# One written order for batch 0 of a hash-masked attention and gated MLP kernel: values up to ten chunks behind scores, exponentials in a ring of nine tiles

## The chip, the core and the metric

The kernel runs on one core of one Trainium2 chip. The metric is the device time of one execution in microseconds (us), lower is better. Engines: PE (matmul), ACT (exponential, gelu, tanh), DVE and POOL (element-wise), SP (issues most DMAs). Each engine runs its own instructions in the order in which the program issues them and waits on semaphores for the others.

## What is computed

```python
# q, k, v: (4, 8, 768, 64); proj: (64, 6)
q_bits = (q @ proj > 0); k_bits = (k @ proj > 0)      # 6 hash bits a token
mask   = bucket(q_bits) == bucket(k_bits)             # equal in all six
scores = where(mask, (q @ k.T) / sqrt(64), -1e9)
attn   = exp(scores - max); attn /= attn.sum() + 1e-9
x      = heads of (attn @ v) side by side             # (3072, 512)
g, val = x @ w_gate, x @ w_val                        # d_ff = 1536
out    = x + sigmoid(x @ w_res) * ((gelu(g) * val) @ w_out)
```

## The kernel before

**Tiling.** Two heads make a *pair* (p = 0 to 15, four pairs a batch, `HP` = 4). A pair's 768 tokens are six tiles of 128. The hash bits are put beside the 64 dimensions as ±0.5, so that one matmul with 71 rows gives a score that is pushed far down wherever the buckets differ, and no mask is applied afterwards. A pair's 2 x 36 score blocks are cut into nine *chunks* of 1024 columns (`NCH` = 9), 36 chunks a batch. Chunks 0 to 3 of a pair need its first head alone, chunk 4 both, 5 to 8 the second alone.

**A chunk.** `scores(p, c)` (L373) is two to four matmuls into a PSUM tile `sp` of 1024 columns (two such buffers, shared with the gate stage) and one exponential on ACT into a tile `e` (L385; pool of four). `values(p, c, e)` (L345) is eight matmuls of 65 columns into the accumulator `av` of a head (two buffers); at the end of a head `preset` (L323) adds a tiny uniform term, and `finish(p, hi)` (L299) divides on DVE into `x_tok`. A finished pair is transposed into `x_sb`, by a DMA on SP's queue (L310) or on PE (`x_turn`, L335).

**Preparing a pair.** Loads on SP (`load`, `load_v`); `tr` (DVE transpose for the hash, L194); `cast` (POOL, into one of four tiles `nat`); `hash_mm` (PE, fp32, L205); `hash_tok` and `bits` (DVE, partly POOL, L215 and L224); then either `turn_pe` and `turned` (PE transposes into a PSUM bank, DVE copy out: pairs 1 to 3) or `turn` (a DMA transpose on SP, L248: pairs 4 to 15), which gives `aug`, the operand of the scores. `vals_a` and `vals_s` prepare the values on POOL.

**Stages.** Per batch: attention (36 slots), then `gate_val(b)` (L403): for m = 0 to 11, eight matmuls with `wg`, eight with `wv` (L399), gelu on ACT (L416), one multiplication on DVE into `hh` (L419). `project(b)` (L425; L431, L445) is a generator whose matmuls are put into the slots of the next batch's attention, or at the end by themselves. Side work of each slot stands in two dictionaries, `side_pe` (issued behind the slot's scores) and `side_work` (issued behind its values); side work of the gate stage stands by m in `gv_work`, issued behind the multiplication of that m. Values come `LAG` = 2 chunks behind scores. The order inside a stage is the order of issue; nothing reorders it later.

**Batch 0** is not covered by a previous batch's projection: its slots hold scores, values, and the preparation of pairs 1 to 3, and its loads come first. In its gate stage pairs 4 to 7 are prepared: `bits` and `turn` of pair 4 and 5 behind m = 0, 1, 2, 4, `tr` of pair 7 behind m = 3 and 5, the hash of pairs 6 and 7 on PE behind m = 6, their `turn`s behind m = 7 to 10. Both loads of pair 7 have been issued in slots 28 and 31 of batch 0. Weight loads are issued on POOL's queue, nine in slots up to 35 and behind m = 0, the others by m = 7.

Of the kernel before, what the change touches and what calls it, by code (L numbers as in the profile page):

```python
# [14 lines left out]


@with_exitstack
def kernel(
# [12 lines left out]
    nc = tc.nc  # L31
# [73 lines left out]
    load(1, 0)  # L105
    load_v(0)
    load(1, 1)
    for p in range(2, 4):
        load_v(p - 1)
        load(p, 0)  # L110
        load(p, 1)
# [76 lines left out]
    t32, hsum, htok = {}, {}, {}  # L188

# [7 lines left out]
    def hash_mm(jobs, dhs=(0, 1), hs_=(0, 1)):  # L197
        if jobs[0] not in hsum:
            hsum[jobs[0]] = mm_ps.tile([P, HT, 32], FP32, tag="r", name="hs")
# [8 lines left out]

    def hash_tok(jobs, psum=False):
        n = 32 * len(jobs)  # L210
        if psum:
            ht = mm_ps.tile([P, HT, 32], FP32, tag="f", name="htp")
        else:
            ht = sm_pool.tile([P, HT, 32], FP32, tag="ht", name="ht")
        nc.vector.transpose(ht[:n].rearrange("p c n -> p (c n)"),  # L215
                            hsum[jobs[0]][:n].rearrange("p c n -> p (c n)"))
        for j, x in enumerate(jobs):
            htok[x] = (ht, j)

    def bits(p, side, engs=(nc.vector,)):  # L220
        x = (p, side)
        ht, j = htok.pop(x)
        for a in range(4):
# [6 lines left out]
    def hash_one(p, side, hi, pool, tag):  # L230
        hs = pool.tile([P, 2, T, 32], FP32, tag=tag, name="hs1")
# [6 lines left out]
    def bits_one(p, side, hi):  # L238
# [4 lines left out]
                                hs[:, 1, :, 0:NBITS], 0.0, 0.5, op0=ALU.is_gt, op1=ALU.subtract)  # L243

# [7 lines left out]

    def turn_pe(p, side, hi, tag=None, pool=mm_ps):
# [3 lines left out]
        pt = pool.tile([P, T, P], BF16, tag=tag or "rf"[side], name="pt")  # L257
# [4 lines left out]
    def turned(p, side, hi, eng, t0=0, t1=T):  # L262
        dst = aug[p, side][0:KA, hi * T + t0:hi * T + t1, :]
        pt = pts[p, side, hi][0:KA, t0:t1]
        if eng is nc.scalar:
            nc.scalar.activation(dst, pt, AF.Copy)
        else:
            eng.tensor_copy(dst, pt)

# [29 lines left out]
    def finish(p, hi):  # L299
# [4 lines left out]
        o = av.pop((p, hi))  # L304
        rec = sm_pool.tile([P, T], FP32, tag="rec", name="rec")
# [3 lines left out]
        if hi == 1 and (0 < b < B - 1 or hp < HP - (2 if b == 0 else 1)):  # L309
# [6 lines left out]
    def opened(p, hi):  # L316
        if (p, hi) in av:
            return
        av[p, hi] = av_ps.tile([P, T + 1, D + 1], FP32, tag="av", name="av")
# [15 lines left out]
    def x_turn(b, hp):  # L335
        pt = mm_ps.tile([P, T, P], BF16, tag="f" if b == 0 else "r", name="pt")
# [8 lines left out]
    def values(p, c, e):  # L345
        va = vaug[p]
        for i in range(2):
# [12 lines left out]
            if (2 * c + i + 1) % NCH == 0:  # L360
                if p < HP:
                    preset(p, hi)
                if (p, hi) not in late:
                    finish(p, hi)

    pending = []
    late = ((0, 0), (0, 1), (1, 0))
# [5 lines left out]
    def scores(p, c):  # L373
# [10 lines left out]
        e = e_pool.tile([P, 1024], BF16, tag="e", name="e")  # L384
# [5 lines left out]
    hidden = {}  # L390
# [12 lines left out]
    def gate_val(b, begun, beside):  # L403
        for m in range(KF):
            ps = []
            for i, w in enumerate((wg, wv)):
# [5 lines left out]
                if m == 0 and i == 1:  # L412
# [4 lines left out]
            if m == 0:  # L417
# [7 lines left out]
    def project(b):  # L425
        hh = hidden[b]
        for t in range(T):
            last = b == B - 1 and t == T - 1
            rps = mm_ps.tile([P, DMODEL], FP32, tag="r", name="rps")
# [8 lines left out]
            for k0, k1 in ((0, 3), (3, 4)) if last else ((0, KM),):  # L438
                cs = slice(k0 * P, k1 * P)
                if b < B - 1:  # L440
                    fps = mm_ps.tile([P, DMODEL], FP32, tag="f", name="fps")
# [22 lines left out]
    tr(0, 0, 1, 2)  # L464
# [44 lines left out]
    for p in range(HP, NPAIR):  # L509
        for hi, s in enumerate((9 * p - (p % HP == 0), 9 * p + 5)):  # L510
            at(s - 2, lambda p=p, hi=hi: opened(p, hi))
# [23 lines left out]


    at(0, lambda: bits_one(0, 0, 1), lambda: tr(1, 0), lambda: bits_one(0, 1, 1))
    pe(0, lambda: hash_one(0, 1, 1, av_ps, "av"))
    at(1, lambda: tr(1, 1))
    pe(2, lambda: turn_pe(0, 0, 1, "av", av_ps), lambda: turn_pe(0, 1, 1))  # L540
    at(2, lambda: turned(0, 0, 1, nc.vector))
    at(2, lambda: turned(0, 1, 1, nc.vector, 0, 2), lambda: turned(0, 1, 1, nc.vector, 2, T))
    at(2, lambda: tr(2, 0))
    hash_pe((1,), 4, (4,))
    turns_pe(1, (6, 6, 8, 9))
    at(6, lambda: finish(0, 0), lambda: tr(2, 1))
    at(8, lambda: tr(3, 0))
    at(9, lambda: tr(3, 1))
    at(11, lambda: finish(0, 1))
    at(5, lambda: vals_a(1))  # L550
    at(7, lambda: vals_s(1))
    for side in range(2):
        at(4 + side, lambda side=side: cast(2, side, nc.gpsimd))
        at(9 + side, lambda side=side: cast(3, side, nc.gpsimd))
    hash_pe((2, 3), 13, (13, 16))
    turns_pe(2, (15, 15, 17, 18))
    at(15, lambda: finish(1, 0))
    at(13, lambda: vals_a(2))
    at(15, lambda: vals_s(2))
    turns_pe(3, (22, 22, 23, 24))  # L560
    at(18, lambda: vals_a(3))
    at(22, lambda: vals_s(3))
    pe(30, lambda: x_turn(0, HP - 2))
    for i in range(6):
        at(11 + 3 * i, load_w)
    for m in (0, 0, 4, 5, 6, 7):
        gv(0, m, load_w)
    loads(0, (3, "v"))

# [4 lines left out]
    for b in range(B - 1):  # L574
# [3 lines left out]
        for j, (x, y) in enumerate(zip(xs, ys)):  # L578
            at(s0 + 24 + 2 * j, lambda x=x: tr(*x))
            at(s0 + 25 + 2 * j, lambda x=x: cast(*x, nc.gpsimd))  # L580
            if j < 2:
                at(s0 + 32 + 2 * j, lambda y=y: tr(*y))
            loads(s0 + (6 if b == 0 else 2) + 4 * j, (x[0], "qk"[x[1]]))
            loads(s0 + (22 if b == 0 else 18) + 3 * j, (y[0], "qk"[y[1]]))
        gv(b, 0, lambda p0=p0: tokens((p0, p0 + 1), True))
# [97 lines left out]
```

## Time and profile before

| | |
|---|---|
| time, median of 3 runs | 346.99 us (346.71 to 347.24) |
| profiled execution: first to last instruction (its span) | 344.9 us |
| median less that span: what lies around it | 2.1 us |
| PE, ACT, DVE, POOL busy | 97%, 60%, 56%, 25% of the span |
| first and last exponential of batch 0 | 8.49 us, 47.47 us (end) |
| gate stage of batch 0, first and last full stretch on PE | 52.25 us to 82.56 us |
| granted PE clock | 1.00 throughout |

The profiled execution has no time of its own beside its span; its own time is taken as the span plus the 2.1 us. Columns of a timeline row: start, us taken, engine, line, operation, output and input, how many, and in brackets the engine's idle time before it with what ended it. Rows of ACT overlap a little when they follow each other closely. A busy PE is not PE at its peak, as the ends of matmuls are modelled: where PE waits is read from the chain of waits.

### The profile page before, as it was taken

The page shows a single profiled execution, that of the slowest core. Times are in us where ns is not written, and L with a number is a line of the kernel's source. Part 1 is how long each engine was busy: PE and PEld are TensorE (multiplying, and loading weights), DVE is VectorE, ACT ScalarE, POOL GpSimd, SP SyncE. Part 2 cuts the span into 40 slices and gives each one's busy share as a digit, 9 for nine tenths or more (in the row PEclk, how much of TensorE's full clock was granted, in tenths as well). Part 3 has the DMA queues.
Part 4 walks back from the last instruction along what each step waited for, and adds up shares of the span by engine and source line. Part 5 has one row for each costly group of instructions (what it writes and reads, how often), then busy time and mean ns, then how long its engine had stood idle before and what let it go on. Part 6 is the DMA issues. An engine that isn't in the chain of part 4 may idle for free.

```text
span 344.9 us, 7549 instructions
## 1 busy us (share of the span) xinstructions
PE 334.2 (97%) x3064; PEld 204.3 (59%) x3112; DVE 191.4 (56%) x403; ACT 206.7 (60%) x232; POOL 86.3 (25%) x162
## 2 busy tenths in 40 slices
PE   7999999999999999999999999999999999999994
PEld 5667665655666655655666665655566665656442
DVE  7877757755345856757344784747244444333333
ACT  3789973226999962224999982323999984223110
POOL 4779940371055000270044100242030000000000
PEclk9999999999999999999999999999999999999999
DMA  7979999999375833528366642626330220000022
GB/s 224 376 62 219 205 276 217 197 139 193 103 188 172 204 106 78 102 38 149 82 193 188 231 115 65 128 48 113 72 100 32 55 55 30 32 1 0 32 77 76
DMA packets 71171, 42.90 MB, mean 124 GB/s; under 512 B 49504, under 2 KB 68192, under 8 KB 71136
## 3 DMA queue, kind: packets, MB, share of 16 engines
q1 hardware_dynamic: 64720, 37.17, 42.9%
q0 software_dynamic: 6336, 5.24, 10.8%
q8 instruction: 24, 0.39, 0.4%
q14 instruction: 11, 0.09, 0.1%
q10 hardware_dynamic: 80, 0.00, 0.0%
HBM read 29.36 MB, written 6.29 MB: 103 GB/s over the span
## 4 chain that ended last, share of the span: by engine, by line
PE 88%; ACT 4%; DVE 2%; DMA 2%; issue 2%; SPq 1%; POOL 0%; DVEq 0%; ACTq 0%
PE sp L399 36%; PE fps L445 18%; PE sp L380 15%; PE av L354 8%; PE rps L431 6%; ACT e L385 4%; PE hs L205 3%; DMA ld<-in_k_dram 2%; PE pt L259 1%; DVE o L451 1%; DVE nat L224 0%; SPq L96 0%; DVE o L448 0%; DVE ht L215 0%; DVE hh L419 0%
## 5 line engine op out<-in xcount | busy, mean ns | idle before, releaser
L385 ACT ACTIVATE e<-sp 128x1024 bf16<-128x1024 f32 x144 | 143.6, 1027 | 13.5 <-PE sp L380 8.0
L416 ACT ACTIVATE gt<-sp 128x768 bf16<-128x768 f32 x48 | 38.9, 811 | 92.5 <-PE sp L399 92.5
L380 PE MATMUL sp<-aug,aug 71*128 71x256 bf16 (+1 forms) x384 | 86.1, 325 | 1.1 <-ACT e L385 0.6
L445 PE MATMUL fps<-wo,hh 128*128 128x512 bf16 (+2 forms) x274 | 74.7, 369 | 1.6
L419 DVE TENSOR_TENSOR hh<-gt,sp 128x768 bf16<-128x768 bf16 x48 | 45.8, 954 | 50.1 <-PE sp L399 46.1
L399 PE MATMUL sp<-x_sb,wv 128*128 128x512 bf16 (+1 forms) x379 | 70.6, 325 | 0.4 <-DVE hh L419 0.2
L399 PE MATMUL sp<-x_sb,wg 128*128 128x256 bf16 (+1 forms) x373 | 70.4, 324 | 0.7
L354 PEld LDWEIGHTS <-e 128*128 128x128 bf16 x1152 | 53.3, 97 | 28.9 <-issue 1.2
L354 PE MATMUL av<-va,e 128*128 128x65 bf16 x1152 | 58.7, 193 | 0.1
L399 PEld LDWEIGHTS <-wv 128*128 128x128 bf16 x384 | 37.6, 98 | 25.1 <-issue 0.3
L399 PEld LDWEIGHTS <-wg 128*128 128x128 bf16 x384 | 36.8, 98 | 26.2 <-issue 2.3
L445 PEld LDWEIGHTS <-hh 128*128 128x128 bf16 x300 | 27.4, 97 | 22.7 <-issue 0.2
L448 DVE SCALAR_TENSOR_TENSOR o<-th,fps 128x512 f32<-128x512 f32 (+2 forms) x25 | 16.6, 666 | 36.6 <-PE fps L445 31.0
L380 PEld LDWEIGHTS <-aug 71*128 71x128 bf16 x384 | 29.4, 97 | 10.9 <-issue 2.2
L184 POOL TENSOR_SCALAR nat<-ld 128x768 bf16<-128x768 f32 (+1 forms) x16 | 13.8, 861 | 78.0 <-DMA aug<-nat 74.6
L281 POOL TENSOR_TENSOR v<-ldv 128x384 f32<-128x384 f32 x16 | 16.0, 999 | 67.7 <-DMA ldv<-in_v_dram 67.6
L194 DVE STREAM_TRANSPOSE t<-ld 128x768 f32<-128x768 f32 (+1 forms) x34 | 31.0, 916 | 1.4 <-DMA ld<-in_q_dram 0.7
L333 DVE COPY av<-av 128x390 f32<-128x390 f32 x24 | 13.6, 567 | 29.8 <-PE av L329 29.8
L431 PE MATMUL rps<-wr,x_sb 128*128 128x512 bf16 x90 | 25.3, 378 | 0.2
L435 ACT ACTIVATE th<-rps 128x512 f32<-128x512 f32 x24 | 14.2, 594 | 18.4 <-PE rps L431 18.4
L224 DVE TENSOR_SCALAR nat<-htp 32x72 bf16<-32x72 f32 x96 | 21.9, 229 | 1.8
L307 DVE TENSOR_TENSOR x_tok<-av,rec 128x384 bf16<-128x384 f32 x32 | 17.8, 557 | 1.1
(61 smaller groups left out, 190.7 us busy)
## 6 DMA issues: line engine op xcount, KB each, us to landing
ldv<-in_v_dram SPq DMA_DIRECT2D x16, 384.0 KB, 5.4
out_dram<-o SPq DMA_DIRECT2D x23, 256.0 KB, 2.0
ld<-in_q_dram SPq DMA_DIRECT2D x15, 384.0 KB, 5.4
ld<-in_k_dram SPq DMA_DIRECT2D x15, 384.0 KB, 6.2
wg<-in_moe_w_gate_dram POOLq DMA_DIRECT2D x4, 384.0 KB, 10.2
wv<-in_moe_w_val_dram POOLq DMA_DIRECT2D x4, 384.0 KB, 12.2
wo<-in_moe_w_out_dram POOLq DMA_DIRECT2D x3, 512.0 KB, 6.9
wr<-in_moe_w_res_dram POOLq DMA_DIRECT2D x1, 512.0 KB, 14.9
```

The costliest lines, as they stand in the source:

```text
L194: nc.vector.transpose(t32[p, side][:, sl].rearrange("p c h n -> p (c h n)"), raw[p, side][:, sl].rearrange("p c d -> p (c d)"))
L224: engs[a % len(engs)].tensor_scalar(nat_of(x)[32 * a:32 * a + 32, :, D:D + NBITS], ht[32 * j:32 * j + 32, :, NBITS * a:NBITS * (a + 1)], 0 ...
L307: nc.vector.tensor_mul(x_tok[b][:, hp, :, hi * D:(hi + 1) * D], o[:, 0:T, 0:D], rec.unsqueeze(2).to_broadcast([P, T, D]))
L354: nc.tensor.matmul(av[p, hi][:, qt, :], e[:, off:off + P], va[:, hi, jt, 0:D + 1], start=first, stop=(p >= HP and jt == T - 1), skip_group ...
L380: nc.tensor.matmul(sp[:, off:off + nq * P], ks[0:KA, hi * T + jt, :], qs[0:KA, hi * T + qt0:hi * T + qt0 + nq, :], start=True, stop=True)
L385: nc.scalar.activation(e, sp, AF.Exp, scale=float(ALPHA))
L399: nc.tensor.matmul(sp[:, c0:c1], w[:, kk, bass.ts(m, P)], xs[:, kk, c0:c1], start=(kk == 0), stop=(kk == KM - 1))
L416: nc.scalar.activation(gt, sp[:, 0:S], AF.Gelu)
L419: nc.vector.tensor_mul(hidden[b][:, m, :], gt, ps[1][:, 0:S])
L431: nc.tensor.matmul(rps, x_sb[b][:, kk, t, :], wr[:, kk, :], start=(kk == 0), stop=(kk == KM - 1))
L445: nc.tensor.matmul(fps[:, cs], hh[:, m, bass.ts(t, P)], wo[:, m, cs], start=(m == 0), stop=(m == KF - 1))
L448: nc.vector.scalar_tensor_tensor(o[:, cs], th[:, cs], 1.0, fps[:, cs], op0=ALU.add, op1=ALU.mult)
```

## The change

Batch 0 no longer runs in the loop over slots. A list of named pieces, `ORDER`, is read from front to back, and each name issues one piece: `sN` scores of chunk N, `vN` its values, `finPH` the finish, `ldPS`/`lvP` loads (S is 0 for q, 1 for k), `trPS`, `csPS` (cast), `hN0` to `hN3` (quarters of a hash), `tkN` (tokens), `btPS` (bits), `tpPSH`/`tdPSH` (turn on PE and copy), `tuPS` (turn by DMA), `vaP`/`vsP`, `wN` (weight load), `xtP` (x_turn), `opP`/`prP`/`rpP` (open, preset, repeat), `g0`, `g1` (first three quarters of m = 0). `BESIDE` is the same for the gate stage of batch 0, by m. The exponentials of batch 0 go into the tile `hh`, which that batch's gate stage fills later: a ring of nine pieces of 1024 columns, where there were four tiles `e`. PSUM banks of `mm_ps`, with fixed names before, are handed out by a list of free ones. Batches 1 to 3 keep their slots.

```diff
+FIRST_LOADS = [(1, "q"), (0, "v"), (1, "k"), (2, "q"), (2, "k"), (1, "v"), (2, "v"), (3, "k"), (3, "q")]
+HASHES = [(0, (1,)), (1, (2, 3)), (2, (4, 5)), (3, (6, 7))]
+ORDER = """
+trq trk s0 tdq tdk hoq bo0 ho bo1 s1 tr10 s2 tr11 tp011 td011a td011b tp001 v0 td001 v1 s3 h00 h01
+s4 cs21 h02 h03 s5 tr20 ld41 ld40 s6 v2 v3 v4 tr21 s7 tk0 bt10 bt11 tp100 tp110 td100 td110 cs20 s8
+ld50 tp111 s9 tr30 tr31 tp101 td101 fin00 s10 lv3 v5 v6 v7 v8 fin01 s11 va1 vs1 lv4 va2 s12 ld60 h10
+h11 h12 h13 ld61 td111 s13 cs31 v9 s14 v10 v11 v12 s15 cs30 tk1 bt20 bt21 tp210 s16 td210 tp200
+td200 v13 fin10 bt31 s17 ld51 va4 v14 s18 tr50 tp201 w0 w1 w2 bt30 td201 s19 v15 vs2 s20 tp211 cs41
+td211 s21 v16 v17 cs40 s22 tr61 v18 v19 tr40 w3 s23 va3 tp310 td310 tr60 s24 v20 tp300 td300 ld70
+s25 vs3 v21 tp301 td301 s26 vs4 fin11 s27 v22 v23 fin20 tr41 s28 v24 v25 s29 tp311 td311 s30 v26
+fin21 lv6 s31 lv5 cs50 v27 s32 cs51 v28 v29 s33 xt2 v30 tr51 s34 w4 w5 w6 v31 fin30 s35 gelu v32 v33
+v34 g0 v35 fin31 g1 xt3 h20 h21 h22 w7 op40
+"""
+BESIDE = [
+    "h23 tk2 bt41",
+    "tu41 cs61 bt40",
+    "bt50",
+    "tu40 cs60 ld71 tr71",
+    "tr70",
+    "tu50 bt51 w8 w9",
+    "",
+    "w10",
+    "h30 h31 h32 h33 tu51 cs71 tk3 bt60 bt61 tu60 tu61",
+    "pr40 rp40 bt71 tu71",
+    "bt70",
+    "w11 cs70 tu70",
+]
...
-        pt = pool.tile([P, T, P], BF16, tag=tag or "rf"[side], name="pt")
+        pt = pool.tile([P, T, P], BF16, tag=tag or take((p, side, hi)), name="pt")
...
-            rps = mm_ps.tile([P, DMODEL], FP32, tag="r", name="rps")
+            rps = mm_ps.tile([P, DMODEL], FP32, tag=take(), name="rps")
...
-        e = e_pool.tile([P, 1024], BF16, tag="e", name="e")
+        if p < HP:
+            if 0 not in hidden:
+                hidden[0] = hh_pool.tile([P, KF, S], BF16, tag="hh", name="hh")
+            n = (p * NCH + c) % RING
+            e = hidden[0].rearrange("p m s -> p (m s)")[:, n * 1024:(n + 1) * 1024]
+        else:
+            e = e_pool.tile([P, 1024], BF16, tag="e", name="e")
...
     for side in range(2):
         tr(0, side, 0, 1)
         hash_one(0, side, 0, av_ps, "av")
-    tr(0, 0, 1, 2)
     cast(0, 0, nc.scalar, 0, 1)
     cast(0, 1, nc.gpsimd, 0, 1)
     bits_one(0, 0, 0)
     turn_pe(0, 0, 0)
     fill(2, 256)
-    turned(0, 0, 0, nc.scalar)
     bits_one(0, 1, 0)
+    turned(0, 0, 0, nc.scalar, 0, 4)
     turn_pe(0, 1, 0)
-    hash_one(0, 0, 1, av_ps, "av")
-    tr(0, 1, 1, 2)
     turned(0, 1, 0, nc.vector, 0, 2)
-    turned(0, 1, 0, nc.vector, 2, T)
...
+    for name in ORDER.split():
+        first.pop(name)()
...
+            for m, names in enumerate(BESIDE):
+                for name in names.split():
+                    gv(b, m, first.pop(name))
...
-    for s in range(LAST):
+    gate_val(0, begun)
+    mlp.append(project(0))
+    for s in range(NSLOT, LAST):
```

More of the change, by code (lines that the diff above doesn't have):

```diff
@@ L104 @@
     load_head(0, 1, 1, nc.sync)
[L105 to L111, printed above, removed]
+    for what in FIRST_LOADS:
+        load_v(what[0]) if what[1] == "v" else load(what[0], "qk".index(what[1]))
     warm = const.tile([P, P], BF16, name="warm")
@@ L211, in hash_tok @@
         if psum:
[L212 removed]
+            ht = mm_ps.tile([P, HT, 32], FP32, tag=take(("ht", ht_of(jobs))), name="htp")
         else:
@@ L222, in bits @@
         ht, j = htok.pop(x)
+        n, what = ht_left.pop(id(ht))
+        if n > 1:
+            ht_left[id(ht)] = (n - 1, what)
+        else:
+            give(what)
         for a in range(4):
@@ L558, with job @@
[L558 to L568, printed above, removed]
+    first = {}
+    def job(name, fn):
+        first[name] = fn
+    held = []
+    for c in range(HP * NCH):
+        job(f"s{c}", lambda c=c: held.append(scores(*divmod(c, NCH))))
+        job(f"v{c}", lambda: values(*held.pop(0)))
```

196 lines of the change are left out of this document (125 added, 71 removed).

## The prediction

> **What bounds the kernel now.** I read the page first, then the chain of waits, then the timelines of ACT, DVE, PE and SP in the two stages that the change rewrites.
>
> ```profile
> PE 88%; ACT 4%; DVE 2%; DMA 2%; issue 2%; SPq 1%; POOL 0%; DVEq 0%; ACTq 0%
> L385 ACT ACTIVATE e<-sp 128x1024 bf16<-128x1024 f32 x144 | 143.6, 1027 | 13.5 <-PE sp L380 8.0
> ```
>
> Over the whole span PE carries the chain, and ACT's exponentials only 4% of it. All of that share lies in batch 0, so batch 0 has to be read by itself. ACT's timeline of batch 0, with the first gelu behind it:
>
> ```profile
> 8.49 4.08 ACT L385 ACTIVATE e<-sp 128x1024 bf16<-128x1024 f32 x4 [0.89 <-PE sp L380]
> 13.39 1.02 ACT L385 ACTIVATE e<-sp 128x1024 bf16<-128x1024 f32 x1 [0.82 <-PE sp L380]
> 14.95 1.94 ACT L385 ACTIVATE e<-sp 128x1024 bf16<-128x1024 f32 x2 [0.54 <-PE sp L380]
> 17.60 5.64 ACT L385 ACTIVATE e<-sp 128x1024 bf16<-128x1024 f32 x6 [0.71 <-PE sp L380]
> 23.72 1.02 ACT L385 ACTIVATE e<-sp 128x1024 bf16<-128x1024 f32 x1 [0.49 <-PE sp L380]
> 25.30 1.94 ACT L385 ACTIVATE e<-sp 128x1024 bf16<-128x1024 f32 x2 [0.55 <-PE sp L380]
> 27.99 6.55 ACT L385 ACTIVATE e<-sp 128x1024 bf16<-128x1024 f32 x7 [0.76 <-PE sp L380]
> 34.80 2.04 ACT L385 ACTIVATE e<-sp 128x1024 bf16<-128x1024 f32 x2 [0.26 <-PE sp L380]
> 37.00 10.47 ACT L385 ACTIVATE e<-sp 128x1024 bf16<-128x1024 f32 x11 [0.16 <-PE sp L380]
> 51.39 0.81 ACT L416 ACTIVATE gt<-sp 128x768 bf16<-128x768 f32 x1 [1.16 <-PE sp L399]
> ```
>
> These 36 exponentials run from 8.49 to 47.47 us, so the last one starts at 37.00 + 10.47 − 1.03 = 46.44. In the undisturbed run of eleven their pitch is (10.47 − 1.03)/10 = 0.944 us; inside the run of seven it is (6.55 − 1.03)/6 = 0.92. Eight times ACT waited for scores: 0.82 + 0.54 + 0.71 + 0.49 + 0.55 + 0.76 + 0.26 + 0.16 = 4.29 us, of which 3.47 fall behind the fifth exponential (13.39). Check: 31 × 0.944 + 3.47 = 32.7 us against the 33.05 from 13.39 to 46.44. So batch 0 is exponentials at full pitch plus gaps in which PE did something else first. The chain within batch 0 says what:
>
> ```profile
> 11.66 0.84 PE hs L205 x8
> 12.51 0.35 PE av L354 x8
> 12.86 0.44 PE sp L380 x3
> 18.18 0.35 PE pt L259 x6
> 22.05 0.79 PE hs L205 x16
> 23.63 0.83 PE hs L205 x16
> 27.17 0.17 PE av L326
> 27.89 0.24 PE av L354 x8
> 49.81 1.11 PE hs L205 x24
> 50.92 0.45 PE sp L399 x2
> ```
>
> In PE time a chunk's scores cost 0.44, its values 0.24, a preset 0.17, a turn of six transposes 0.35, half a four-job hash about 0.8. The waits of ACT sit where such pieces stand between two chunks' scores. After the last exponential PE needs until 50.92 for the rest of batch 0; from there the gate stage keeps it full.
>
> **Part 1: the order of batch 0.** Moving values does not remove PE work; it moves it out of the crowded slots. Between two scores PE may spend 0.944 − 0.44 = 0.50 us before it is the later of the two. The second `sp` buffer adds a little once: an exponential starts about 0.6 us after its scores begin (12.86 to 13.39 is 0.53), so PE may lag 0.3 to 0.4 before ACT waits. I went through ORDER with the prices above, carrying the lag. Most slots hold 0.24 to 0.6 us of other work and pay the lag back. Five do not: two quarters of a hash behind s4 (0.8), three values and a preset behind s6 (0.9), two turns behind s7 (0.7, which also wait on DVE's tokens and bits), four values and a preset behind s10 (1.15), and four quarters behind s12 (1.6). Their excess over 0.50 plus the lag is about 0.1, 0.2, 0.25, 0.35 and 0.7: 1.6 us of waiting in place of 3.47, a gain of 1.9. From s14 on nothing exceeds it, where the old order still lost 0.55, 0.76, 0.26 and 0.16.
>
> The fifth exponential: in the old order a hash (11.66), then values (12.51), then its scores (12.86). Both values now stand ahead of the hash, so the scores come right behind it, 0.35 earlier. The hash itself keeps its time, since it waits for POOL's copies of `projw`, which stay behind the same cast:
>
> ```profile
> 10.73 0.88 POOL L144 COPY projw<-projn 32x12 f32<-32x12 f32 x4
> 5.03 0.58 DVE L194 STREAM_TRANSPOSE t<-ld 128x384 f32<-128x384 f32 x1 [0.67 <-DMA ld<-in_q_dram]
> 5.53 0.35 DVE L240 STREAM_TRANSPOSE hs<-hs 128x192 f32<-128x192 f32 x1
> ```
>
> Ahead of that, the DVE transpose that waited for its load until 5.03 no longer stands before the first bits (5.53), so the first scores come up to 0.6 earlier; but the second halves' transposes, bits and copies then come later on DVE, and they are what the fifth chunk needs. I count 0.3 gained at the fifth exponential; the ends are 0.6 and −0.5. Sum at the end of batch 0: 1.9 + 0.3 = **2.2 us**. With the pitch 0.92 it is 31 × 0.024 = 0.7 more (2.9); if the gaps stay as large as they are, only 0.3. The tail from the last exponential to the gate stage keeps its pieces.
>
> [...]
>
> **Part 2: the load of pair 7's k.** BESIDE issues `ld71` on SP's queue only behind m = 3, and `tr71`, which reads it, on DVE directly behind it. On SP it stands behind `tu41` and `tu40`; `tu40` waits for `bt40`, the bits behind m = 1. On DVE, queued behind `tr71` is the multiplication of m = 4, and for that PE waits with the `wv` matmuls of m = 5, because it frees their buffer.
>
> ```profile
> 53.73 0.93 DVE L224 TENSOR_SCALAR nat<-htp 32x72 bf16<-32x72 f32 x4
> 56.10 0.95 DVE L224 TENSOR_SCALAR nat<-htp 32x72 bf16<-32x72 f32 x4
> 60.32 0.95 DVE L419 TENSOR_TENSOR hh<-gt,sp 128x768 bf16<-128x768 bf16 x1 [0.66 <-PE sp L399]
> 61.19 0.97 DVE L194 STREAM_TRANSPOSE t<-ld 128x768 f32<-128x768 f32 x1
> 62.92 0.95 DVE L419 TENSOR_TENSOR hh<-gt,sp 128x768 bf16<-128x768 bf16 x1 [0.76 <-PE sp L399]
> 63.95 1.46 PE L399 MATMUL sp<-x_sb,wv 128*128 128x512 bf16 x8
> ```
>
> In the old trace's times (all of this shifts together): bits of m = 0 end at 54.66, those of m = 1 at 57.05. The multiplication of m = 3 starts at 60.32, a transpose behind it at 61.19, that of m = 4 at 62.92 and ends at 63.87; PE wants the buffer at 63.95. There is no slack there. A transpose of 0.97, less the 0.08 by which DVE's rows overlap (60.32 + 0.95 against 61.19), holds the next one off by 0.89, so the load must have landed by 62.92 − 0.89 = 62.03. When does it?
>
> ```profile
> 54.82 3.77 SPq L248 DMA_TRANSPOSE aug<-nat  x1
> 82.10 1.43 SPq L248 DMA_TRANSPOSE aug<-nat  x1
> 83.58 0.91 SPq L78 DMA_DIRECT2D ld<-in_q_dram  x1
> ld<-in_q_dram SPq DMA_DIRECT2D x1, 384.0 KB, 5.8
> DMA to landing us min/median/max: 4.0/4.0/4.0
> DMA to landing us min/median/max: 3.4/3.4/3.4
> DMA to landing us min/median/max: 7.1/11.4/16.1
> q0 software_dynamic: 1852, 1.58, 98.4%
> ```
>
> A turn leaves SP 0.16 us after its bits (54.66 to 54.82) and occupies SP for 1.43 us when the DMAs are quiet (82.10), 3.77 when they are not (54.82). So `tu40` goes at 57.2 and `ld71` at 58.7. A load right behind a turn landed 5.8 us after issue in batch 1 (83.58; the fourth line) and 4.0 in batch 2 (the fifth, the load at 163.6); one at 98.3 took 3.4; among weight loads they took 7.1 to 16.1 (the seventh, loads from 24 to 39 us). Landing at 62.1, 62.7 or 64.5 stalls PE by 0.1, 0.7 or 2.5 us, once, and PE is full from there to the end of the stage, so it is lost. I take 1.5, between the two that stood behind a turn.
>
> **Part 3: edits at nothing.** The exponentials in `hh`: its first piece is overwritten by m = 0, long after the values that read it (v27), and its last one by m = 11, after v35; if the order did not cover it, one value step (0.24). The banks from a list: the order of rps and fps stays alternating. The hash of pairs 6 and 7 moves from m = 6 to m = 8: PE pays it there instead; behind it DVE has tokens and two sets of bits, 0.6 + 2 × 0.95 = 2.5 us, while PE's hash and m = 9 take over 3; no stall, or 0.3 if it slips. Weight loads go out later: the last two pairs of `wg`, `wv` slices only near s34, needed at m = 6 and 9; `wr` and `wo` behind cs60, needed in batch 1, some 15 us on. The last of these is the nearest: POOL can ask for `wr` when `tu40` has landed and cs60 is done, some 5 to 8 us behind 57.2;
>
> ```profile
> wr<-in_moe_w_res_dram POOLq DMA_DIRECT2D x1, 512.0 KB, 14.9
> ```
>
> with the 14.9 us that it took among the other weights it lands by 62 to 65 + 15 = 80 at the latest, and the gate stage ends at 82.5. If it were later still, the first slots of batch 1 would wait for the difference.
>
> **Sum.** Span 344.9 − 2.2 + 1.5 = 344.2; with the 2.1 us around it 346.3, against the median 346.99.
>
> **The rivals.**
>
> *Full gain.* The load lands by 62.1, as the load at 98.3 would (3.4), and batch 0 gains 2.2 to 2.9: 346.99 − 2.5 = 344.5. For it: DMAs have less to do in batch 0. Against: the two loads behind a turn took longer. [...] Chance 0.20.
>
> *Late load, slower than before.* When `tu41` leaves, slices of the weights asked for at s34 are still in flight, as in the old trace, where the software queue had 98.4% of the engines from 50 to 60 us. Then `tu41` takes 3.77 (to 58.6), `tu40` 1.43 (60.1), `ld71` lands at 65.9 and PE stalls 3.9 us: 346.99 − 2.2 + 3.9 = 348.7; if both turns and the load are slowed, 5 us and more, 350. It decides from a stall of 2.2, a landing at 64.3. For it: the row of 54.82. Against: only the four slices asked for last are behind, and no loads. Chance 0.20.
>
> *Batch 0 does not tighten.* DVE, with `tr20`, `tr21` and tokens in one row behind s5, or a POOL waiting for `lv4` (which SP issues only behind the DMA of pair 0's x), holds the turns up, and the gaps move rather than go: gain 0.5, stall 1.5: 348.0. Chance 0.15; the ring and the lag of ten chunks then do nothing, since nothing but PE's order was to be gained by them.
>
> **How the numbers follow.** My case (gain 2.2, stall 1.5) has 0.45 and spans 345.0 to 347.6 by itself. What a measurement here tells from no change is about 0.2%, 0.7 us, so faster means under 346.3, which is where my own figure lies. Faster: half of my case 0.23 and the full gain 0.20, 0.43. Same: 0.16 of my case and 0.04 of the last, 0.20. Slower: 0.06, 0.20 and 0.11, 0.37. The range 344.4 to 349.0 leaves out the best part of the full gain (0.08) and the worst of the late load (0.1).
>
> **What would show it.** Right: in the new trace the last exponential of batch 0 starts near 44.2, ACT's gaps sum to about 2 us and sit behind chunks 4 to 12; in the gate stage DVE's transpose of m = 3 waits for the DMA of `ld`, and PE has one pause of about 1.5 us before the `wv` matmuls of m = 5. Wrong: gaps behind s14 (ACT is not held by PE's order), no pause at m = 5 (rival one), a pause above 2.2 us (rival two), or pauses at another m or in the first slots of batch 1, which I have priced at nothing.

## The result, and the profile after

| | before | after |
|---|---|---|
| time, median (runs) | 346.82 us (12, 346.42 to 347.46) | 346.1 us (12, 345.6 to 347.14) |
| ratio | | 0.9982 (95%: 0.9974 to 0.999) |
| span of the profiled execution | 344.9 us | 344.4 us |
| first and fifth exponential | 8.49, 13.39 | 8.50, 13.89 |
| first gelu of batch 0 | 51.39 | 50.85 |
| table load behind the gate stage of batch 0 | 82.12 | 82.17 |

The changed kernel is faster by 0.18%. The forecast was 346.3. One slow run, 352.66 us in the experiment e2_bits_behind, is left out of its ratio. Read between the marks of the table, the half microsecond of span is the sum of four parts, and no part has the size that was forecast: the fifth exponential comes 0.50 later, the stretch from there to the first gelu is 1.04 shorter (38.00 to 36.96), the gate stage 0.59 longer (30.73 to 31.32), and everything behind it 0.55 shorter (262.78 to 262.23).

First the timeline of ACT after the change, to be held against the one of before in the prediction (columns: start, us taken, engine and line, what, how many; in brackets the idle time before it and what ended it):

```profile
8.50 1.02 ACT L459 ACTIVATE hh<-sp 128x1024 bf16<-128x1024 f32 x1 [1.04 <-PE sp L448]
10.44 1.94 ACT L459 ACTIVATE hh<-sp 128x1024 bf16<-128x1024 f32 x2 [0.92 <-PE sp L448]
12.58 1.02 ACT L459 ACTIVATE hh<-sp 128x1024 bf16<-128x1024 f32 x1 [0.19 <-PE sp L448]
13.89 1.02 ACT L459 ACTIVATE hh<-sp 128x1024 bf16<-128x1024 f32 x1 [0.29 <-PE sp L448]
15.21 5.83 ACT L459 ACTIVATE hh<-sp 128x1024 bf16<-128x1024 f32 x6 [0.29 <-PE sp L448]
21.45 1.94 ACT L459 ACTIVATE hh<-sp 128x1024 bf16<-128x1024 f32 x2 [0.41 <-PE sp L448]
23.86 8.55 ACT L459 ACTIVATE hh<-sp 128x1024 bf16<-128x1024 f32 x9 [0.47 <-PE sp L448]
33.78 13.16 ACT L459 ACTIVATE hh<-sp 128x1024 bf16<-128x1024 f32 x14 [1.37 <-PE sp L448]
...
50.85 0.81 ACT L489 ACTIVATE gt<-sp 128x768 bf16<-128x768 f32 x1 [1.16 <-PE sp L472]
```

Seven waits behind the fifth exponential have become four, 0.29 + 0.41 + 0.47 + 1.37 = 2.54 us in place of 3.47. But more than half of that is one wait of 1.37 ahead of chunk 22, in a part of the order for which the prediction saw none; a gap behind s14 was the first sign that it had named for being wrong. DVE's timeline ahead of it, and PE's row:

```profile
28.07 0.90 DVE L282 TENSOR_SCALAR nat<-ht 32x72 bf16<-32x72 f32 x2
28.99 0.98 DVE L240 STREAM_TRANSPOSE t<-ld 128x768 f32<-128x768 f32 x1
29.98 2.21 DVE L282 TENSOR_SCALAR nat<-ht 32x72 bf16<-32x72 f32 x4
32.22 1.02 DVE L329 COPY aug<-pt 71x768 bf16<-71x768 bf16 x2
...
33.30 0.39 PE L448 MATMUL sp<-aug,aug 71*128 71x512 bf16 x1 [1.20 <-DVE aug L329]
```

PE stops in the middle of chunk 22's scores, because the copy of `td211` (the second of the two at 32.22) is not there. On DVE that copy stood behind half of `bt31`, `tr50` and `bt30`. The four bits of `bt30` took 2.21 us. A narrower window gives the last two of them alone, and POOL's timeline what ran beside:

```profile
30.60 1.59 DVE L282 TENSOR_SCALAR nat<-ht 32x72 bf16<-32x72 f32 x2
...
30.34 0.75 POOL L193 DMA_DIRECT2D wg<-in_moe_w_gate_dram  x1
31.10 1.02 POOL L346 TENSOR_TENSOR v<-ldv 128x384 f32<-128x384 f32 x1
```

They end at 32.19, and POOL's addition beside the last one ends at 31.10 + 1.02 = 32.12.

Second, the load that was moved behind m = 3. The timelines of SP, DVE and PE in the gate stage, and the line of that load's landing:

```profile
54.27 3.58 SPq L308 DMA_TRANSPOSE aug<-nat  x2
57.91 0.89 SPq L107 DMA_DIRECT2D ld<-in_k_dram  x1
...
62.10 0.98 DVE L240 STREAM_TRANSPOSE t<-ld 128x768 f32<-128x768 f32 x1 [1.36 <-DMA ld<-in_k_dram]
63.00 0.92 DVE L492 TENSOR_TENSOR hh<-gt,sp 128x768 bf16<-128x768 bf16 x1
...
62.11 1.46 PE L472 MATMUL sp<-x_sb,wg 128*128 128x512 bf16 x8
63.97 1.46 PE L472 MATMUL sp<-x_sb,wv 128*128 128x512 bf16 x8 [0.39 <-DVE hh L492]
```

```profile
DMA to landing us min/median/max: 4.2/4.2/4.2
```

DVE's transpose waits 1.36 for the load, the multiplication of m = 4 comes behind it, and the `wv` matmuls of m = 5 start 1.86 behind the `wg` matmuls where the matmuls before and after are 1.30 apart: 0.56 us lost, at the place that was named. That eats the 0.54 won in batch 0, so that both kernels end the gate stage at the same time.

### The profile page after: what moved, and what is told of

It is laid out like the page before. It is cut to its first block, busy times and chain, and to the rows that moved or that the text cites. A ratio compares the mean times of both kernels' runs of the same rounds, so it can differ in the third digit from the quotient of the medians.

```text
span 344.4 us, 7546 instructions
## 1 busy us (share of the span) xinstructions
PE 333.5 (97%) x3064; PEld 204.3 (59%) x3112; DVE 191.7 (56%) x404; ACT 206.2 (60%) x232; POOL 85.6 (25%) x162
## 4 chain that ended last, share of the span: by engine, by line
PE 90%; DVE 3%; ACT 3%; issue 1%; DMA 1%; SPq 0%; POOL 0%; DVEq 0%; ACTq 0%; POOLq 0%
PE sp L472 34%; PE fps L518 18%; PE sp L448 17%; PE av L421 9%; PE rps L504 6%; PE hs L251 3%; ACT hh L459 2%; DMA ld<-in_k_dram 1%; PE pt L320 1%; PE wps L174 1%; DVE nat L282 1%; PE hs L293 1%; DVE aug L329 1%; ACT gt L489 0%; SPq L308 0%
## 5 line engine op out<-in xcount | busy, mean ns | idle before, releaser
L459 ACT ACTIVATE e<-sp 128x1024 bf16<-128x1024 f32 x108 | 109.0, 1028 | 8.0 <-PE sp L448 2.8
L472 PE MATMUL sp<-x_sb,wv 128*128 128x256 bf16 (+1 forms) x378 | 70.6, 325 | 0.7 <-DVE hh L492 0.4
L421 PEld LDWEIGHTS <-e 128*128 128x128 bf16 x864 | 40.2, 97 | 25.1
L421 PE MATMUL av<-va,e 128*128 128x65 bf16 x864 | 43.4, 193 | 0.0
L459 ACT ACTIVATE hh<-sp 128x1024 bf16<-128x1024 f32 x36 | 34.4, 1026 | 5.1 <-PE sp L448 5.0
L521 DVE SCALAR_TENSOR_TENSOR o<-th,fps 128x512 f32<-128x512 f32 (+2 forms) x25 | 16.7, 666 | 36.9 <-PE fps L518 30.0
L210 POOL CAST nat<-ld 128x768 bf16<-128x768 f32 (+1 forms) x17 | 13.3, 783 | 39.7 <-DMA aug<-nat 38.8
```

Of the source, the lines that this page charges most:

```text
L421: nc.tensor.matmul(av[p, hi][:, qt, :], e[:, off:off + P], va[:, hi, jt, 0:D + 1], start=first, stop=(p >= HP and jt == T - 1), skip_group ...
L459: nc.scalar.activation(e, sp, AF.Exp, scale=float(ALPHA))
L472: nc.tensor.matmul(sp[:, c0:c1], w[:, kk, bass.ts(m, P)], xs[:, kk, c0:c1], start=(kk == 0), stop=(kk == KM - 1))
L521: nc.vector.scalar_tensor_tensor(o[:, cs], th[:, cs], 1.0, fps[:, cs], op0=ALU.add, op1=ALU.mult)
```

## The experiments

Each kernel is the changed one with one edit, the last two with two and three; all were timed against the kernel before on their own chip (346.81, 346.94 and 347.02 us there), and ratios are against that. The changed kernel was not timed again beside them, so where an edit is set against it, the two ratios are compared (its own is 0.9982). Batch 0 shifts with the landing of the first loads (the first exponential came between 7.91 and 9.49), so stages are compared by their lengths. The changed kernel's marks are: fifth exponential to first gelu 36.96, fifth exponential to table load 68.28.

### The load

**e1_load_early** issues it where the second load of batch 0's end stands:

```diff
-fin21 lv6 s31 lv5 cs50 ...                 # ORDER
+fin21 lv6 s31 lv5 ld71 cs50 ...
-    "tu40 cs60 ld71 tr71",                  # BESIDE, m = 3
+    "tu40 cs60 tr71",
```

> The changed kernel with one name moved: ld71, the load of pair 7's k, goes out behind lv5 (slot 31) and no longer behind m = 3. If the pause of 0.56 us before the wv matmuls of m = 5 is that load and is lost for good: no wait of DVE's transpose on a DMA there, gate stage of batch 0 back to 30.3 us, 0.56 us less than the changed kernel, about 345.5. If instead something behind it is late anyway (the turns of pair 5, the weight slices that the load now meets): the pause moves to another m and the time stays at 346.1.

344.91 us (5 runs), ratio 0.9951 (0.9939 to 0.9963). PE's timeline at m = 5, and ACT's table load:

```profile
61.67 1.46 PE L472 MATMUL sp<-x_sb,wg 128*128 128x512 bf16 x8
62.97 1.46 PE L472 MATMUL sp<-x_sb,wv 128*128 128x512 bf16 x8
...
81.17 1.28 ACT L459 ACT_TABLE_LOAD   x1
```

No pause: 1.30 from one to the next. The late load is the cause: in the ten traces that keep it PE waits at this place (0.27 to 0.67 us), in the three with the early one it does not. The ratio falls by 0.0031, 1.1 us, which is more than the pause. From the fifth exponential (13.79) to the table load it is 67.38, 0.90 less: 0.56 by the pause, 0.34 because the wait at chunk 22 was 1.03 in this execution. There the two bits of `bt31` on DVE took 0.56 us, where the row at 28.07 above has 0.90.

### The wait ahead of chunk 22

Theory: DVE's queue sets it. Four edits change what stands in it or how long it takes.

**e2_bits_behind** moves `tr50` and `bt30` on DVE behind the copy that PE wants:

```diff
-... s18 tr50 tp201 w0 w1 w2 bt30 td201 s19 v15 vs2 s20 tp211 cs41 td211 s21
+... s18 tp201 w0 w1 w2 td201 s19 v15 vs2 s20 tp211 cs41 td211 tr50 bt30 s21
```

> The changed kernel with tr50 and bt30 moved on DVE from slot 18 to behind td211 (slot 21), so that the two copies for which the scores of chunk 22 wait no longer stand behind them. If DVE's queue makes ACT's gap of 1.37 us at 33.78: the gap shrinks to 0.2 or less, the last exponential of batch 0 starts 1.2 us earlier (44.7), time about 344.9. If PE's own work is as full as ACT's there: the gap comes back in smaller pieces by slot 35, time 345.6 to 346.1.

347.71 us (11 runs), ratio 1.0027 (1.0016 to 1.0038): slower than the changed kernel, which both sides had missed. ACT's timeline shows where the gain went:

```profile
37.71 2.02 ACT L459 ACTIVATE hh<-sp 128x1024 bf16<-128x1024 f32 x2 [1.09 <-PE sp L448]
40.22 7.49 ACT L459 ACTIVATE hh<-sp 128x1024 bf16<-128x1024 f32 x8 [0.49 <-PE sp L448]
```

The wait at chunk 22 is gone, and 1.09 + 0.49 come back at chunks 26 and 28: the same DVE work now stands ahead of pair 3's turns. Here work moved within a full queue moved the wait. The trace does not account for the whole loss: first gelu is 37.34 behind the fifth exponential, 0.38 more than in the changed kernel, while the ratio is 0.0045 higher, 1.6 us. The traced execution was one of the quicker ones (347.08), and four of the ten runs in the ratio had a mean granted clock of 0.994 or 0.995, where it had 0.997; what they lost, and where, no trace shows.

**e3_vsum_early** takes POOL's additions away from beside the bits:

```diff
-... s17 ld51 va4 v14 s18 ... s19 v15 vs2 s20
+... s17 ld51 vs2 va4 v14 s18 ... s19 v15 s20
```

> The changed kernel with one name moved: vs2 (POOL's sums over the values of pair 2) from slot 19 to ahead of va4 in slot 17, where POOL waited 1.7 us for a load. bt30 then no longer runs beside POOL's additions. If DVE's small operations are slowed by POOL's tensor operations beside them (four took 2.21 us where four took 0.93 elsewhere, the last one 1.06 while POOL's addition took 1.02): bt30 takes 1.2 us or less, the gap of 1.37 shrinks to about 0.4, time about 345.2. If they are slowed by POOL's weight loads or by themselves: bt30 stays near 2.2 and the time at 346.1.

346.96 us (11 runs), ratio 1.0006 (0.9997 to 1.0015), worse than the changed kernel's 0.9982. DVE's and POOL's rows, and PE's wait:

```profile
30.18 2.22 DVE L282 TENSOR_SCALAR nat<-ht 32x72 bf16<-32x72 f32 x4
...
30.76 0.75 POOL L193 DMA_DIRECT2D wg<-in_moe_w_gate_dram  x1
31.50 0.84 POOL L210 CAST nat<-ld 128x768 bf16<-128x768 f32 x1
...
33.51 0.39 PE L448 MATMUL sp<-aug,aug 71*128 71x512 bf16 x1 [1.45 <-DVE aug L329]
```

The bits are as slow (2.22), with a DMA issue and a cast beside them instead of the additions. So it is not one POOL operation that slows them. The two bits of `bt31` ahead of them took 1.14 here, 0.24 more than in the changed kernel, and ACT's wait at chunk 22 is 1.62, 0.25 more.

**e11_tokens_psum** leaves POOL's other work as it is and puts the input of those bits into PSUM; all bits of pairs 2 and 3 then stand on DVE, four more in all:

```diff
-job(f"tk{n}", lambda ps=ps: tokens(ps, ps[0] >= HP))
+job(f"tk{n}", lambda ps=ps: tokens(ps, ps[0] >= 2))
-... (nc.vector,) if side == 0 or p >= HP else (nc.gpsimd, nc.vector)
+... (nc.vector,) if side == 0 or p >= 2 else (nc.gpsimd, nc.vector)
```

> The hash tokens of pairs 2 and 3 go to PSUM instead of SBUF, and their bits stand wholly on VectorE (GpSimd did half of the k side's). [...] Then every set of four bits of pairs 2 and 3 takes 0.90 to 0.98 us, pair 3's q bits too (2.21 in the changed kernel), though GpSimd's operations lie beside it as before; the gap behind chunk 21 shrinks from 1.37 to below 0.7 and the time is 345.3 to 346.1. Rival: the bits are held by GpSimd's work wherever their input lies (the output is in SBUF still): single bits of 0.4 to 1.06 us remain, and with two more bits a set on VectorE the time is 346.1 to 347.

346.68 us (11 runs), ratio 0.9993 (0.9984 to 1.0001). The groups of bits by line between 23 and 33 us, those of pairs 2 and 3 (columns: how many, ns shortest/median/longest, first and last start), first of the changed kernel, then of this one, and of this one its last eight bits, POOL's rows beside them, and a row of PE:

```profile
L282 DVE TENSOR_SCALAR nat<-ht x12: 185/202/1061, 23.9 to 31.1; 32x72 bf16<-32x72 f32 x12
```

```profile
L282 DVE TENSOR_SCALAR nat<-htp x16: 221/228/239, 24.6 to 32.3; 32x72 bf16<-32x72 f32 x16
```

```profile
29.56 0.98 DVE L282 TENSOR_SCALAR nat<-htp 32x72 bf16<-32x72 f32 x4
...
31.55 0.96 DVE L282 TENSOR_SCALAR nat<-htp 32x72 bf16<-32x72 f32 x4
...
29.89 0.75 POOL L193 DMA_DIRECT2D wv<-in_moe_w_val_dram  x1
...
31.39 1.01 POOL L346 TENSOR_TENSOR v<-ldv 128x384 f32<-128x384 f32 x1
...
32.55 0.50 PE L320 MATMUL pt<-ident,nat 128*71 128x128 bf16 x6 [0.77 <-DVE nat L282]
```

The place of the input decides here: with a DMA issue and an addition on POOL beside them no bit takes over 239 ns, where single bits with their input in SBUF took up to 1061. The time is not better than the changed kernel's, since DVE has more bits and PE now waits for those (0.77 at 32.55); first gelu 37.12 behind the fifth exponential. The first of the two times expected was missed at its upper end, the rival's met, but for another reason than the rival's.

**e7_bits_pool** takes `bt30` off DVE: POOL makes pair 3's q bits, directly behind its half of the k bits.

```diff
-td200 v13 fin10 bt31 s17 ... w0 w1 w2 bt30 td201
+td200 v13 fin10 bt31 bt30 s17 ... w0 w1 w2 td201     # bt30 on nc.gpsimd
```

> The changed kernel with all four parts of bt30 on POOL, right behind its parts of bt31, where POOL stood idle for 1.7 us; none left on DVE. If ACT's gap of 1.37 us is DVE's queue (bt30 of 2.21 us ahead of the copies for chunk 22): the copies come at 30.0, the gap goes to 0.2 or less and does not come back at chunk 27, last exponential of batch 0 at 44.7, time about 344.9. If the weight loads, 0.4 later on POOL, or PE's own work hold it then: 345.5 to 346.1.

345.04 us (6 runs), ratio 0.9947 (0.9932 to 0.9962). ACT:

```profile
13.88 1.02 ACT L459 ACTIVATE hh<-sp 128x1024 bf16<-128x1024 f32 x1 [0.29 <-PE sp L448]
...
23.84 21.71 ACT L459 ACTIVATE hh<-sp 128x1024 bf16<-128x1024 f32 x23 [0.47 <-PE sp L448]
...
49.47 0.81 ACT L489 ACTIVATE gt<-sp 128x768 bf16<-128x768 f32 x1 [1.16 <-PE sp L472]
```

23 exponentials without a wait, the whole second part of batch 0, at (21.71 − 1.03)/22 = 0.94 us each; first gelu 35.59 behind the fifth exponential, 1.37 less than in the changed kernel, which is the size of the wait. DVE's queue was the cause.

### How far the values lag

**e5_lag2** puts each values step two chunks behind its scores, **e12_lag3** at most three; in both the finish of pair 1's second head stands earlier, because the two accumulators then need it. In the order as it is the distance reaches five (`v5` behind `s10`, `v22` behind `s27`); title and prediction overstated it with ten.

```diff
-... s10 lv3 v5 v6 v7 v8 fin01 s11 ... s21 v16 v17 cs40 s22 ...
+... s10 lv3 v8 fin01 s11 ... s21 cs40 v19 s22 ...      # two chunks, every values step so
+... s10 lv3 v7 v8 fin01 s11 ... s21 cs40 v18 s22 ...   # at most three
```

> The changed kernel with the values of batch 0 two chunks behind the scores, as before, instead of up to ten (fin11 moved forward to suit); everything else in its place. If the lag is what batch 0 lives on: slots with turns or hashes take a value step more, ACT's gaps behind the fifth exponential grow from 2.8 us to well over 3.5, and the time is 346.8 or more. If the gaps are set by DVE's queue and by the places of hashes and turns, and the values fit anywhere: gaps grow by 0.2 to 0.4 us (the prediction's own prices give 0.2), time 346.1 to 346.5.

> Values at most three chunks behind their scores instead of up to five; all else in the order as it is. Theory: what the distance buys is that copies, bits and finishes on VectorE are not queued behind work that waits for late scores and values; two chunks cost 5 us, so three cost something between, 347 to 350 us, and ScalarE's gaps behind the fifth exponential sum to 3 to 4.5 us (2.54 in the changed kernel, 5.14 with two). Rival, the price of the prediction (values are only PE time, 0.24 us each, and cost where a slot is overfull): 346.1 to 346.4, gaps of 2.5 to 2.8.

Two chunks: 351.1 us (4 runs), ratio 1.0115 (1.0102 to 1.0128). Three: 347.52 us (12 runs), ratio 1.0015 (1.0005 to 1.0024). The changed kernel has 0.9982. ACT's waits behind the fifth exponential sum to 0.54 + 0.20 + 1.20 + 1.71 + 0.25 + 1.24 = 5.14 with two and 0.29 + 0.95 + 1.17 + 0.84 = 3.25 with three, against 2.54. Of three, ACT's rows and one of PE:

```profile
23.82 8.75 ACT L459 ACTIVATE hh<-sp 128x1024 bf16<-128x1024 f32 x9 [0.95 <-PE sp L448]
...
38.38 9.50 ACT L459 ACTIVATE hh<-sp 128x1024 bf16<-128x1024 f32 x10 [0.84 <-PE sp L448]
...
37.57 0.28 PE L421 MATMUL av<-va,hh 128*128 128x65 bf16 x4 [0.52 <-DVE x_tok L373]
```

With three, first gelu comes 38.28 behind the fifth exponential, 1.32 later than in the changed kernel. The wait ahead of chunk 13, at the hash of pairs 2 and 3, is 0.95 for 0.47, but the 0.41 ahead of chunk 11 is gone; that exponential comes 10.30 behind the fifth, where it came 9.97 behind it. One values step, `v9`, has moved into that full slot, so these 0.33 are near the prediction's own price of 0.24. The rest comes behind chunk 22, and most of it is not PE's time: ACT waits 0.84 ahead of chunk 26, because a values step waits for an accumulator that a finish on DVE has not yet given back. With two chunks something else comes in. PE's longest wait, and the five microseconds behind it by the view of windows (window, its length, busy time and instructions of five engines, then granted clock, DMA share, GB/s):

```profile
35.36 0.39 PE L448 MATMUL sp<-aug,aug 71*128 71x512 bf16 x1 [1.74 <-DVE aug L329]
```

```profile
36.00:41.00 5.00, 5.00 (x53) 3.74 (x52) 3.24 (x6) 3.52 (x4) 4.68 (x10) 0.66 1.61 137
37.00:40.00 3.00, 3.00 (x22) 1.93 (x21) 1.93 (x4) 1.81 (x2) 2.84 (x7) 0.50 1.35 135
```

A wait of 1.74 that ends at 35.36, and from 36.9 to 40.3 PE runs at half its clock; ACT's waits of 0.25 and 1.24 are of that stretch. What it withholds is 5 × (1 − 0.66) = 1.7 us of PE at full clock, or 3.4 us at half. All four runs of this kernel have a mean clock of 0.989 to 0.993. So of the 3.27 by which first gelu is farther from the fifth exponential (40.23), at most about half belongs to the half clock and the rest to the distance itself.

### The start and the loads

**e4_old_start** gives the changed kernel the start of before, with the second halves' transposes and one hash ahead of the first exponential:

```diff
-trq trk s0 tdq tdk hoq bo0 ho bo1 s1 tr10 ...
+s0 ho bo0 tr10 bo1 s1 ...                  # tr and hash_one back ahead of s0
```

> The changed kernel with the start of the kernel before: second halves of pair 0 transposed and hashed ahead of the first scores, copies whole. If the new start costs the first five exponentials (second one 1.03 us later, fifth 13.89 against 13.39): the fifth comes at 13.1 to 13.4, time about 345.5. If the fifth hangs on POOL's copies of projw, which came 0.8 later because the load of pair 1's q landed later: it stays near 13.8 and the time at 346.1.

346.66 us (12 runs, 345.41 to 349.06), ratio 1.0003 (0.9985 to 1.002): not told apart from before or from the changed kernel. The profiled execution was the longest of these; it and the next (348.69) had a mean granted clock of 0.992 and 0.993, the other ten at least 0.997. The fifth exponential and PE's wait at chunk 22, then the window behind that wait:

```profile
14.33 1.02 ACT L459 ACTIVATE hh<-sp 128x1024 bf16<-128x1024 f32 x1 [0.29 <-PE sp L448]
...
34.12 0.49 PE L448 MATMUL sp<-aug,aug 71*128 71x512 bf16 x1 [1.58 <-DVE aug L329]
```

```profile
34.00:38.00 4.00, 3.88 (x38) 2.79 (x39) 2.88 (x5) 2.12 (x3) 3.99 (x8) 0.57 1.28 192
```

The fifth exponential stands 14.33 − 9.49 = 4.84 behind the first, as in the kernel before (4.90), where the changed one takes 5.39. The old start is quicker by 0.5 between these marks, but its first exponential came at 8.97 and 9.49 in two traces (8.49 in the kernel before), where the new start had it between 7.91 and 9.23; so part of that may have been paid ahead of it. And the wait at chunk 22 was 1.58 in this execution, and the clock fell behind it as in e5_lag2: 4 × (1 − 0.57) = 1.7 us withheld. Behind waits of 1.20, 1.33 and 1.45 (the changed kernel, three chunks, e3_vsum_early) the clock of batch 0 stayed at 1.00.

**e8_old_loads** goes back to the old order of the first loads:

```diff
-FIRST_LOADS = [(1, "q"), (0, "v"), (1, "k"), (2, "q"), (2, "k"), (1, "v"), (2, "v"), (3, "k"), (3, "q")]
+FIRST_LOADS = [(1, "q"), (0, "v"), (1, "k"), (1, "v"), (2, "q"), (2, "k"), (2, "v"), (3, "q"), (3, "k")]
```

> The changed kernel with the order of the first loads of the kernel before (v of pair 1 ahead of q and k of pair 2, q of pair 3 ahead of k). If the order made the loads ahead of it land later (q of pair 1 at 6.5 before, at 8.7, 8.6, 7.1 and 8.6 in four traces with the new order): q of pair 1 lands near 6.5 again, POOL's projw copies come 0.8 earlier, the fifth exponential at 13.3 or earlier, time 345.6. If the landing is chance or the fifth exponential hangs on DVE (copies of the second halves): 346.1, or later by what DVE then waits for q and k of pair 2.

346.13 us (12 runs), ratio 0.9979 (0.9968 to 0.9989); the fifth exponential again 5.39 behind the first. The order of these loads is worth nothing that shows. Nor do POOL's copies of `projw` hold the fifth exponential here. They were done at 11.55, and the hash that needs them (first row; the second is that of the changed kernel) came only when PE had got to it:

```profile
13.13 0.84 PE L251 MATMUL hs<-t,projw 128*32 128x192 f32 x8
...
12.47 0.84 PE L251 MATMUL hs<-t,projw 128*32 128x192 f32 x8
```

In e1_load_early the copies were the later of the two (the hash waited 0.43 for them), and there the fifth exponential came 5.88 behind the first.

### The banks

**e6_fixed_banks** gives the PSUM banks their old fixed names from batch 1 on:

```diff
-pt = mm_ps.tile([P, T, P], BF16, tag=take(), name="pt")
+pt = mm_ps.tile([P, T, P], BF16, tag="r" if later else take(), name="pt")
...                                          # hs in the same way, htp with "f"
-rps = mm_ps.tile([P, DMODEL], FP32, tag=take(), name="rps")
+rps = mm_ps.tile([P, DMODEL], FP32, tag="r", name="rps")
...                                          # fps with "f"
```

> The changed kernel with the fixed bank names of the kernel before from batch 1 on (rps, hash and last x_turn in r, fps and tokens in f). If the 0.43 us that the new trace gains behind batch 0 (0.2 near 115 us, 0.3 near 304 us) came from the banks: time 346.5, and the two pauses are back. If they were accidents of the one execution: time 346.1, as the changed kernel.

345.89 us (6 runs), ratio 0.9964 (0.995 to 0.9978): no loss without the list, so the list does not make the gain behind the gate stage. From the table load to the end this kernel takes 262.4 us, the others of this study 262.1 to 262.7, the changed one 262.2 and the kernel before 262.8. The 0.55 there is within what executions differ by; its cause stays open.

### Both repairs, and the old start with them

**e9_load_pool** is e1_load_early and e7_bits_pool together; **e10_load_pool_start** has the old start too.

> Two edits at once: the load of pair 7's k issued right behind the loads of pair 5's v, and pair 3's q bits wholly on GpSimd behind the k bits. Theory: the two losses are separate (one is VectorE's queue in batch 0, the other the landing of one load in the gate stage), so their gains add: about 346.1 - 1.2 - 1.1 = 343.8 us, the first gelu near 49.5, no pause above 0.2 us ahead of the wv matmuls of m = 5, the table load behind the gate stage near 80.3. Rival: both runs profited from the same thing (the gate stage's start, or a luckier landing of the first loads), so the two together give no more than one of them: 344.9 to 345.0.

> The two edits of the run before this, and the old start: the first two transposes and hash_one pieces of pair 0's second halves stand where the kernel before had them, ahead of the first exponential. Theory: the new start costs 0.5 us between the first and the fifth exponential (5.39 against 4.90 us), because both hash_one pieces stand between the first and second chunk's scores; with the old start the fifth comes 4.8 to 4.9 behind the first, the gap behind the first exponential goes, and the time is 343.3 us. Rival: the first exponential itself comes later by as much, since a transpose that waits for its load stands ahead of the first bits: 343.8, as without the edit, or up to 0.5 more.

344.69 us (5 runs), ratio 0.9935 (0.9923 to 0.9947), and 344.42 us (5 runs), ratio 0.9927 (0.9914 to 0.9939). ACT of the first, then of the second:

```profile
14.16 1.02 ACT L459 ACTIVATE hh<-sp 128x1024 bf16<-128x1024 f32 x1 [0.29 <-PE sp L448]
...
80.52 1.28 ACT L459 ACT_TABLE_LOAD   x1
```

```profile
8.97 3.03 ACT L459 ACTIVATE hh<-sp 128x1024 bf16<-128x1024 f32 x3 [1.04 <-PE sp L448]
...
13.81 1.02 ACT L459 ACTIVATE hh<-sp 128x1024 bf16<-128x1024 f32 x1 [0.29 <-PE sp L448]
...
80.16 1.28 ACT L459 ACT_TABLE_LOAD   x1
```

From the fifth exponential to the table load it is 66.36, 1.92 less than in the changed kernel: 1.37 (the wait at chunk 22) and 0.56 (the pause) add up. The forecast of 343.8 was too low because it took e1's whole gain for the pause's. In the time itself the ratio falls by 0.0047, 1.6 us. The old start brings the fifth exponential 4.84 behind the first instead of 5.39 and drops the 0.92 wait behind the first exponential; the table load is 0.36 earlier, but the two times' intervals overlap, so on the clock this last 0.3 us is not shown. Both versions beat both kernels: 2.3 and 2.6 us under 347.02.

## Why the prediction was right, and where its steps were not

**The sum held because its errors cancelled.** Forecast span 344.2, measured 344.4: batch 0 gained 1.66 less than the 2.2 forecast, the pause cost 0.94 less than 1.5, and 0.55 came from behind the gate stage, where no step was. That three misses left only 0.2 us is luck, and the third of them is of the size by which executions differ. The 2.1 us around the span was wrong too: the profiled execution of the changed kernel took 346.07 for 344.4, so 1.7 lie around it; 2.1 had been got from the span of one execution and the median of others.

**Part 1, the gaps** (1.9 forecast, 3.47 − 2.54 = 0.93 measured). Slot by slot the five places were priced at 0.1, 0.2, 0.25, 0.35 and 0.7; the trace has 0.29, 0, 0, 0.41 and 0.47 there. That pricing, on PE's time, was fair: 1.17 for 1.6. The step that failed is "From s14 on nothing exceeds it". Only PE had been carried through ORDER, and the engine that decides there is DVE, whose copies stand behind bits, transposes and finishes. Nor would the one price that it had for a set of bits, 0.93 to 0.95 from the gate stage, have done in batch 0: there the input is `htp` in PSUM, here `ht` in SBUF. The kernel before had shown it (the group of bits by line in its batch 0):

```profile
L224 DVE TENSOR_SCALAR nat<-ht x18: 185/194/759, 14.7 to 30.3; 32x72 bf16<-32x72 f32 x18
```

A longest of 759 ns beside a median of 194 was the sign to look at. The third rival named DVE, with `tr20`, `tr21` and tokens behind s5; its mechanism came, seventeen slots later, and its gain of 0.5 was the size. Its other wait, a POOL that stands until `lv4` has landed, is seen (POOL's cast at 27.81 waited 1.70 for a load of values) but held up no turn.

**The fifth exponential** (0.3 earlier forecast, 0.50 later measured, the lower end given). The reason given for that end is what happened: the second halves' transposes now come behind the first scores, both hashes of those halves stand between the first two chunks' scores on PE, and ACT waits 0.92 for the second. The step that failed is "The hash itself keeps its time, since it waits for POOL's copies": it started at 12.47 for 11.66, and e8_old_loads shows PE itself as the later of the two. The old start takes the 0.92 away (4.84 for 5.39 from first to fifth). The 0.50 as such is one execution against another: the fifth exponential came between 13.52 and 14.62 in the eleven traces with the new start, and at 13.39, 13.81 and 14.33 in the three with the old.

**The distance of the values** got no price of its own in the sum; the third rival even allowed that ring and distance do nothing. With three chunks the time is 1.1 us worse (ratios 1.0015 and 0.9982), with two 4.6, part of that by the clock. So with at most three chunks this order would have been slower than the kernel before. Part of the price is PE's, near 0.24 for a step in an overfull slot, and part is DVE's, as above.

**Part 2, the load** (1.5 forecast, 0.56 measured). Mechanism, place and bounds were right. Landing took 4.2, next to the lower of the two rows quoted (4.0 and 5.8), where the value taken lay between them. In the old trace's times, with batch 0 ending 0.54 earlier, the load came at 57.91 + 4.2 + 0.54 = 62.65, and the prediction's own conversion gives 0.7 for a landing at 62.7; 0.56 was lost. So the conversion held and the landing was mis-sized: 4.2 us, where 1.5 of pause stands for 4.8. The other 0.25 us of the miss is the issue, which came at 58.45 in those times, where 58.7 was forecast. The rival of full gain took the 3.4 of the load at 98.3, which leaves 0.1 of pause; the measured 4.2 speaks against it. The late load of the second rival did not come: SP issued both turns in 3.58 us, where that rival had 3.77 + 1.43.

**Part 3** held: no pause elsewhere in the gate stage, and none at m = 8 or in the first slots of batch 1; the banks move nothing.

## What to carry to other kernels

Carry every engine's queue through a new order, not only that of the engine which the chain of waits names: here PE's gaps shrank, and DVE's order then made the longest wait, 1.37 us. The price of an operation went with the memory its input lay in and with what the neighbouring engine did meanwhile (bits of 221 to 239 ns from PSUM, of 185 to 1061 from SBUF beside POOL), so take it from the same stage, and look at the longest beside the median. An order that merely moved work within a full queue moved the wait (1.37 at chunk 22 became 1.09 and 0.49 in e2_bits_behind); it took another engine (e7_bits_pool, no wait there) or an earlier issue (e1_load_early, no pause at m = 5) to remove one.

## What the runs showed of the hardware

**Bits with their input in SBUF were held up beside POOL's work.** The twelve bits of 32 x 72 of pairs 2 and 3 in the changed kernel took 185 to 1061 ns, with a median of 202: 0.69 us beside a cast on POOL (28.07), 0.40 beside a DMA issue (29.98), 1.06 beside an addition (31.13), where the bit ended 0.07 us behind POOL (32.19 and 32.12). Not every bit beside a DMA issue was held: one at 30.40 took 0.19. With the input in PSUM all sixteen of e11_tokens_psum took 221 to 239 ns, eight of them beside POOL's DMA issues and addition. How POOL's work holds a bit up, and what POOL does in a DMA issue, no row shows.

**PE's clock fell to half behind a wait of 1.58 us.** Behind waits of 1.58 and 1.74 us (e4_old_start, e5_lag2) the granted clock fell to 0.50, 0.2 and 1.5 us after PE had resumed. Ahead of them it was 1.00, with PE busy for 1.92 of 2.00 us (30 to 32) and for all of 3.50 (30 to 33.5). In both executions 1.7 us were withheld, that is 3.4 us at half clock; behind 1.20, 1.33 and 1.45 it stayed at 1.00. The length of the wait is not all that decides. At the ends of the traces, where PE has no more to do, the clock fell 3.0 us behind the last matmul in the changed kernel (339.92 and 342.96), and in the kernel before it was still 1.00 at the end of the span, 4.5 us behind it (340.44 and 344.9). So the traces give no limit between 1.45 and 1.58, and no run here varied the place of the wait by itself; what else decides stays open.
